# A retention block and a SoLU layer on one core: the state decays once every second chunk, and one written order replaces start, loop and end

## The chip, the core and the metric

The kernel runs on one core of one Trainium2 chip. The core has a matrix engine (PE, whose weight loads are shown apart as PEld), a vector engine (DVE), an activation engine (ACT), a general engine (POOL) and a queue engine (SP), which here issues nearly all DMAs. Each engine works through its own instructions strictly in the order in which they were written; engines wait for one another by semaphores. The metric is the device time of one execution in microseconds (us). The time before is the median of three runs, 217.87 us (217.39 to 219.24).

## What is computed

```python
def _attn_ref(q, k, v):                      # 8 batches, 8 heads, 576 tokens, 64 wide
    scores = scale * np.matmul(q, k.transpose(0, 1, 3, 2))
    gamma = 1.0 - 2.0 ** (-5.0 - np.arange(H, dtype=np.float32))
    Dmat = np.where(rel >= 0, gamma[:, None, None] ** rel[None, :, :], 0.0)
    return np.matmul(scores * Dmat[None, :, :, :], v)
...
def _moe_ref(x, w_in, w_out, g_ln):          # x: 4608 x 512, w_in: 512 x 1024
    h = x @ w_in
    sm = softmax(h)                          # over the 1024
    solu = h * sm
    ln = (solu - mean) / np.sqrt(var + 1e-06) * g_ln
    return ln @ w_out
```

(The softmax is written out in the reference with its maximum, exponential and sum.) All inputs and the output are float32.

## The kernel before

**Tiles.** The 4608 tokens are 36 chunks of 128. A group of nine chunks serves two batches: chunks 0 to 7 of a group are four chunks of each batch, taken in turn, and the ninth holds the last 64 tokens of both. So chunk n has the place c = (n mod 9) // 2 in its batch, and c = 4 for the ninth. The retention is computed chunk by chunk: scores inside the chunk, under a mask, plus the product of the queries with a state that is carried from chunk to chunk of the same batch. The powers of gamma are not put on the scores: q is multiplied by gamma to the position and v by gamma to minus the position (tables in `small`), so that their product has gamma to the distance, and the mask is only a triangle of ones. Positions are counted inside the chunk, so the state has to be multiplied by gamma to the 128 whenever a chunk is passed.

**Steps.** The work on chunk n is cut into named steps. A token `mx:1` in the order calls step `mx` for chunk 1; a letter behind it chooses an engine (`a` ACT, `v` DVE, `g` POOL).

- `ld` three loads q, k, v (L185, L192, on SP). `cq` scales q (L210, or L199 for chunk 34), `cv` scales v (L199), `ck` copies k to 16 bits (L171).
- `tq` eight PE transposes of q and k (L232) and `eq` two copies out of PSUM (L171). From chunk 12 on, for c < 4, `tr` turns q alone (L256), `er` copies it, and `kd` turns k by a DMA transpose (L241).
- `sc` scores (L290), `mk` two masked copies `ret` on DVE (L303), `av` scores times v into `x` (L365).
- `kv` the chunk's k-v product (L314), `ad` adds it to the carried state: `t` (a copy at L327 for c = 0, else the sum at L329, on DVE). `dk` on POOL (L341) makes `s16`, the decayed 16-bit state that the next chunk of the batch multiplies with, `d3` on POOL (L353) the decayed 32-bit state `s32` that the next `ad` adds to. `fs` adds q times `s16` into `x` (L380); for c = 0 there is no state and it issues nothing.
- `ex` copies `x` to `xT` (L171). `m1` (or four quarters `mr` for the first two chunks, L400) is `h = x w_in` (L412), eight matmuls of 512 columns. `mx` the negated row maximum on DVE (L422), `xp` the exponential on ACT (L428), `so` the product on DVE (L437), `ce` a centring for the first five chunks (L448, L453), `sq` the sum of squares on ACT.
- `rt` three tiny POOL instructions (L477, then L481 or L483, then the power at L487) that give 1/sqrt(var). `tu` eight PE transposes (L495) with the copy `eu` (L171), or for seven late chunks `du`, a DMA transpose (L500). `m2` eight matmuls with w_out (L515), `st` the scaled copy on ACT (L523) and the store on SP (L528).
- Set-up steps: `li`, `wi` load and convert w_in, `lo`, `wo` w_out, `mm`, `mc`, `ws` subtract its column mean; `c1` makes constants and loads the tables, `wu` is four matmuls on zeros. The last chunk goes in halves (`hm`, `hx`, `hp`, `ho`, `hc`, `ht`, `he`, `hq`, `h2`, `hw`).

**Order.** Nothing is scheduled by a program at this point: the strings START, LOOP (run for i = 7 to 27, numbers counted from i) and END are the order of every engine's queue. BANKS says which of four PSUM bank slots each PE step takes, in the same order; `h` has two slots of its own. A step that takes a slot waits until its last reader is done. The part of START that the prediction walks through begins with `mx:1`:

```
mr:1:1 mr:0:0 mr:0:2 mk:2 ck:4:g mx:1 xp:1 mr:0:1 mr:0:3 av:2 dk:1 mx:0 tq:4 eq:4:a so:1 cv:4:g
ce:1 wu:0:4 fs:2 lo:1 lo:2 cq:3:v sc:4 ex:2:a ck:3:g cv:3:g tu:1 xp:0 mk:4 m1:2 sq:1 tq:3 eu:1:a
...
wo:0:a sq:0 d3:5 av:6 sq:2 mx:5 fs:6 ck:7:g mm:0 m2:1 cq:7:g ld:9 mx:3 eu:0:a rt:2 mc:0:v m2:0
ce:4 cq:8:v ws:3:v rt:0 xp:3 tu:4 ex:6:a ws:7:v ld:10 ws:4:v ck:8:g dk:5 st:1 xp:5 tq:7 sq:4
so:3 eu:4:v ld:11 eq:7:a m2:2 st:0 so:5 tq:8 ce:3 eq:8:a m1:6 ws:1:v ws:0:v cv:7:g sc:7 ws:2:g
```

and the loop is

```
tr:2 so:-1 tu:-2 ld:6 er:2:v m1:0 dk:0 kv:1 eu:-2:a kd:4 ad:1 cv:3:g av:1 mx:0 sc:2 sq:-2 fs:1
ex:1:a rt:-2 cq:4:g xp:0 m2:-2 d3:0 ck:5:g st:-2 mk:2
```

Of the kernel before, what the change touches and what calls it, by code (L numbers as in the profile page):

```python
# [22 lines left out]
START = """
ld:0 ld:1 c1:0 ck:0:g cq:0:v cv:0:v li:3 gt:0 c2:0 tq:0 cq:1:g cv:1:v ld:2 kv:0 ck:1:v tq:1 ad:0
eq:1:a d3:0 cq:2:v cv:2:g li:2 li:0 eq:0:a kv:1 wi:3:1:a sc:1 li:1 mk:1 dk:0 sc:0 ck:2:a ld:4
av:1 wi:3:0:a wi:2:1:g fs:1 tq:2 ld:3 mk:0 ad:1 av:0 ex:1:a wi:0:0:g eq:2:a fs:0 wi:1:1:a kv:2
mr:1:3 ad:2 d3:1 wi:1:0:g wi:2:0:v cq:4:g wi:0:1:v d3:2 sc:2 mr:1:0 ex:0:v ld:5 mr:1:2 ld:6  # L30
mr:1:1 mr:0:0 mr:0:2 mk:2 ck:4:g mx:1 xp:1 mr:0:1 mr:0:3 av:2 dk:1 mx:0 tq:4 eq:4:a so:1 cv:4:g
ce:1 wu:0:4 fs:2 lo:1 lo:2 cq:3:v sc:4 ex:2:a ck:3:g cv:3:g tu:1 xp:0 mk:4 m1:2 sq:1 tq:3 eu:1:a
dk:2 kv:4 eq:3:a ck:5:a kv:3 av:4 cq:5:g so:0 fs:4 ad:3 d3:3 sc:3 mx:2 dk:3 cq:6:g ex:4:a mk:3
ad:4 tq:5 cv:5:g xp:2 eq:5:a m1:4 lo:0 lo:3 sc:5 d3:4 so:2 cv:6:g mk:5 dk:4 kv:5 av:3 ck:6:a
fs:3 tq:6 d3:6 wo:4:g av:5 ex:3:a ld:7 eq:6:a wo:1:g mx:4 ad:5 wo:7:g kv:6 xp:4 m1:3 fs:5 ce:0
ce:2 wo:2:a ex:5:a tu:0 tu:2 sc:6 wo:5:a m1:5 ld:8 ad:6 so:4 wo:3:a eu:2:v mk:6 rt:1 wo:6:v
wo:0:a sq:0 d3:5 av:6 sq:2 mx:5 fs:6 ck:7:g mm:0 m2:1 cq:7:g ld:9 mx:3 eu:0:a rt:2 mc:0:v m2:0
ce:4 cq:8:v ws:3:v rt:0 xp:3 tu:4 ex:6:a ws:7:v ld:10 ws:4:v ck:8:g dk:5 st:1 xp:5 tq:7 sq:4
so:3 eu:4:v ld:11 eq:7:a m2:2 st:0 so:5 tq:8 ce:3 eq:8:a m1:6 ws:1:v ws:0:v cv:7:g sc:7 ws:2:g
tu:3 st:2 rt:4 ws:5:v ld:12 m2:4 mk:7 sc:8 sq:3 eu:3:a cq:9:g mx:6 mk:8 m2:3 st:4 dk:6 rt:3  # L40
cq:10:g kv:7 ck:9:a ws:6:v xp:6 cv:9:v ad:7 cv:8:v st:3 av:7 fs:7 ex:7:a ck:10:a ck:11:a
"""
# [4 lines left out]
END = """
d3:-7 tr:-5 kd:-3 cq:-3:g kv:-6 av:-6 er:-5:v ld:-1 ad:-6 tr:-4 fs:-6 ex:-6:a dk:-7 sq:-9
so:-8 sc:-5 m1:-7 cv:-4:g er:-4:v mk:-5 tr:-3 kd:0 kv:-5 ck:-2:g av:-5 sq:-8 fs:-5 tu:-8 mx:-7
ad:-5 rt:-9 cv:-3:g dk:-5 er:-3:a tu:-9 kd:-2 m1:-6 xp:-7 sc:-4 kv:-4 cq:-2:v eu:-9:v so:-7  # L50
ex:-5:a m1:-5 sc:-3 mk:-4 rt:-8 du:-7 d3:-6 ld:0 mx:-6 eu:-8:a d3:-5 mk:-3 ad:-4 ck:-1:a dk:-6
m2:-9 av:-4 mx:-5 xp:-6 kv:-3 av:-3 d3:-4 cv:-1:g st:-9 d3:-1 ad:-3 kd:-1 cv:-2:g d3:-2 cq:0:g
fs:-4 fs:-3 so:-6 tr:-2 er:-2:v ex:-4:a xp:-5 m2:-8 sq:-6 dk:-4 sc:-2 mk:-2 ck:0:g m1:-4 so:-5
kv:-2 kv:-1 du:-5 ex:-3:a av:-2 sq:-7 st:-8 mx:-4 sq:-5 xp:-4 fs:-2 m1:-3 cq:-1:v cv:0:g kq:-1
rt:-5 dk:-3 ex:-2:a d3:-3 ad:-2 du:-6 tr:0 so:-4 er:0:a m2:-7 sc:0 m1:-2 ad:-1 mk:0 mx:-3
sc:-1 rt:-6 mk:-1 mx:-2 m2:-5 sq:-4 du:-4 kv:0 rt:-7 rt:-4 av:-1 av:0 fs:-1 dk:-1 m2:-6 st:-7
xp:-3 so:-3 ex:-1:v xp:-2 so:-2 du:-3 du:-2 dk:-2 sq:-3 st:-6 fs:0 m1:-1 rt:-3 ex:0:a st:-5
sq:-2 hm:0:0 hm:0:1 m2:-3 mx:-1 hx:0:0 hx:0:1 xp:-1 hp:0:1 so:-1 m2:-2 hp:0:0 ho:0:1 ho:0:0
du:-1 ht:0:1 hc:0 st:-3 ht:0:0 m2:-4 he:0:1:v sq:-1 hq:0:0:v he:0:0:v rt:-2 rt:-1 ad:0
hq:0:1:a h2:0:0 rt:0 m2:-1 h2:0:1 st:-4 st:-2 hw:0:0:a st:-1 hw:0:1:v  # L60
"""
# [32 lines left out]
def kernel(  # L94
# [61 lines left out]
    gq, gk = small[:, 0:8], small[:, 8:16]  # L156
    gqt, gkt = small[:, 16:24], small[:, 24:32]
    gs = small[:, 32:36]
    gd = small[:, 36:44].rearrange("p (a b) -> p a b", a=4)
    gqm = small[:, 44:52]  # L160
# [43 lines left out]

    def cq(n, e="g"):
        if not quads(n):
            return scaled(n, "qf", "q16", gq, ENG[e])
        table = gqm if chunks[n][1] == 4 else gqt
        dst = half.tile([P, H, D], F16, name="q16", bufs=5)
        ENG[e].tensor_tensor(  # L210
            out=dst.rearrange("p (a h) d -> p h a d", h=2),
            in0=T.pop(("qf", n)).rearrange("p (h a) d -> p h a d", h=2),
            in1=table.rearrange("p (h a) -> p h a", h=2).unsqueeze(3).to_broadcast([P, 2, 4, D]),
            op=ALU.mult,
        )
        T["q16", n] = dst
# [88 lines left out]

    def kv(n):

        k16, v16 = T.pop(("k16", n)), T["v16", n]
        if chunks[n][1] == 4:
            return  # L310
        kp = bank([P, 4, D], FP, "kp")
        for hp in range(4):
# [5 lines left out]
        T["kp", n] = kp

    def ad(n):  # L320
# [1 line left out]
        if chunks[n][1] == 4:  # L322
            return
        (b,), c = chunks[n]
        t = stp.tile([P, 4, D], FP, name="t")
        if c == 0:
            nc.vector.tensor_copy(out=t, in_=T.pop(("kp", n)))  # L327
        else:
            nc.vector.tensor_tensor(  # L329
                out=t, in0=T.pop(("kp", n)), in1=T.pop(("s32", b, c)), op=ALU.add  # L330
            )
        T["t", n] = t

    def dk(n):

# [4 lines left out]
        s16 = stp.tile([P, 4, 2, D], F16, tag=f"s16_{b % 2}", name="s16")  # L340
        nc.gpsimd.tensor_tensor(  # L341
            out=s16, in0=t.unsqueeze(2).to_broadcast([P, 4, 2, D]),
            in1=gd.unsqueeze(3).to_broadcast([P, 4, 2, D]), op=ALU.mult,
        )
        T["s16", b, c + 1] = s16

    def d3(n):

        if chunks[n][1] >= 3:
            return  # L350
        (b,), c = chunks[n]
        s32 = stp.tile([P, 4, D], FP, tag=f"s32_{b % 2}", name="s32")
# [4 lines left out]

    def av(n):

        ret, v16 = T.pop(("ret", n)), T.pop(("v16", n))  # L360
        x = bank([P, 4, P], FP, "x")

        for hp in range(4):
            for e in range(2):
# [5 lines left out]
        T["x", n] = x  # L370

    def fs(n):

        bs, c = chunks[n]
        qkT = T.pop(("qkT", n))
        s16 = [T.pop(("s16", b, c)) for b in bs] if c > 0 else []
        w = P // len(bs)
        for hp in range(4):
            for i, s in enumerate(s16):
# [88 lines left out]
            )  # L468
        T["ss", n] = ss

    def rt(n):

        w1 = tiny.tile([P, 1], FP, name="w1")
        w2 = tiny.tile([P, 1], FP, name="w2")
        rs = tiny.tile([P, 1], FP, name="rs")
        s = T.pop(("s", n))
        nc.gpsimd.tensor_scalar(  # L477
            out=w1, in0=s, scalar1=s, scalar2=1e-6 * DFF, op0=ALU.mult, op1=ALU.mult
        )
        if n < PLAIN:  # L480
            nc.gpsimd.tensor_tensor(out=w2, in0=w1, in1=T.pop(("ss", n)), op=ALU.add)  # L481
        else:
            nc.gpsimd.tensor_scalar(  # L483
                out=w2, in0=T.pop(("ss", n)), scalar1=1.0 / DFF**2, scalar2=w1, op0=ALU.mult,
                op1=ALU.add,
            )
# [248 lines left out]
    def run(order, base):  # L735

        for token in order.split():
            name, n, *more = token.split(":")
            n = base + int(n)
            if 0 <= n < NCH:  # L740
                step[name](n, *more)

    with tc.manual_schedule():
        run(START, 0)
        for i in range(FIRST, STOP - STEP + 1, STEP):
            run(LOOP, i)
        run(END, NCH - 1)


# [28 lines left out]
```

## Time and profile before

| | us |
|---|---|
| three runs: median (lowest to highest) | 217.87 (217.39 to 219.24) |
| the profiled execution: its own time | 218.18 |
| its span in the profile | 216.5 |
| PE busy, share of the span | 197.4, 91% |
| DVE busy | 180.8, 84% |
| POOL busy | 173.6, 80% |
| ACT busy | 167.1, 77% |

The profile is of one execution. Its own time is 1.7 us longer than the span, which runs from the first to the last instruction. Busy time is the union of an engine's instructions; on DVE, ACT and PE an instruction starts a little before the one ahead of it has ended, so the step from one start to the next is shorter than the duration (a DVE maximum lasts 1.22 us and the next instruction starts 1.14 us after it). In a timeline each row has its start, its duration, the engine, the line, the operation and what is written and read.

### The profile page before, as it was taken

The page shows a single profiled execution, that of the slowest core. Times are in us where ns is not written, and L with a number is a line of the kernel's source. Part 1 is how long each engine was busy: PE and PEld are TensorE (multiplying, and loading weights), DVE is VectorE, ACT ScalarE, POOL GpSimd, SP SyncE. Part 2 cuts the span into 40 slices and gives each one's busy share as a digit, 9 for nine tenths or more (in the row PEclk, how much of TensorE's full clock was granted, in tenths as well). Part 3 has the DMA queues.
Part 4 walks back from the last instruction along what each step waited for, and adds up shares of the span by engine and source line. Part 5 has one row for each costly group of instructions (what it writes and reads, how often), then busy time and mean ns, then how long its engine had stood idle before and what let it go on. Part 6 is the DMA issues. An engine that isn't in the chain of part 4 may idle for free.

```text
span 216.5 us, 5376 instructions
## 1 busy us (share of the span) xinstructions
PE 197.4 (91%) x1989; PEld 110.8 (51%) x1989; DVE 180.8 (84%) x289; ACT 167.1 (77%) x279; POOL 173.6 (80%) x275
## 2 busy tenths in 40 slices
PE   0379889896999999999999999999999999999993
PEld 0254456453455555555555555555555565545451
DVE  1378899999997998888888898888888999889840
ACT  2073988966897888888888788888888794986991
POOL 3348889997367899999997899999997899977340
PEclk9999999999999999999999999999999999999999
DMA  5999999998986899799999998899999999674845
GB/s 137 289 317 287 228 280 358 193 245 224 270 228 168 219 183 201 177 225 258 243 223 232 255 208 186 186 247 248 214 227 213 253 181 190 145 172 100 195 109 182
DMA packets 112250, 47.04 MB, mean 217 GB/s; under 512 B 96984, under 2 KB 106208, under 8 KB 112224
## 3 DMA queue, kind: packets, MB, share of 16 engines
q1 hardware_dynamic: 111904, 46.55, 92.7%
q8 instruction: 15, 0.25, 0.5%
q10 hardware_dynamic: 320, 0.16, 0.3%
q14 instruction: 11, 0.09, 0.2%
HBM read 32.54 MB, written 9.44 MB: 194 GB/s over the span
## 4 chain that ended last, share of the span: by engine, by line
PE 78%; DVE 13%; DMA 2%; issue 2%; SPq 2%; ACT 1%; DVEq 0%; ACTq 0%
PE o L515 26%; PE h L412 23%; PE sc L290 5%; PE lp L495 5%; PE x L365 4%; PE x L380 3%; PE kp L314 3%; DVE nm L422 3%; DVE ret L303 2%; DMA vf<-in_v_dram 2%; PE tp L232 2%; PE tr L256 2%; PE h L400 2%; DVE u L437 2%; DVE q L210 1%
## 5 line engine op out<-in xcount | busy, mean ns | idle before, releaser
L412 PE MATMUL h<-w_in,xT 128*128 128x512 f16 x264 | 62.4, 379 | 0.5 <-DVE u L437 0.5
L515 PE MATMUL o<-w_c,uT 128*128 128x512 f16 x240 | 56.5, 379 | 0.6 <-DVE t L327 0.4
L428 ACT ACTIVATE e<-h,nm 128x1024 f32<-128x1024 f32 x35 | 39.0, 1116 | 14.0 <-DVE nm L422 14.0
L303 DVE TENSOR_TENSOR ret<-sc,tris 128x512 f16<-128x512 f32 x72 | 46.1, 682 | 1.3 <-PE sc L290 1.2
L437 DVE SCALAR_TENSOR_TENSOR u<-h,e 128x1024 f16<-128x1024 f32 x35 | 42.7, 1220 | 2.7 <-ACT e L428 1.4
L422 DVE TENSOR_REDUCE nm<-h 128x1 f32<-128x1024 f32 x35 | 42.5, 1216 | 2.0 <-PE h L412 1.5
L515 PEld LDWEIGHTS <-uT 128*128 128x128 f16 x280 | 26.2, 98 | 27.1 <-issue 0.4
L412 PEld LDWEIGHTS <-xT 128*128 128x128 f16 x264 | 24.2, 98 | 24.4 <-issue 0.5
L341 POOL TENSOR_TENSOR s<-t,small 128x512 f16<-128x512 f32 x32 | 34.2, 1070 | 2.6 <-DVE t L329 2.6
L199 POOL TENSOR_TENSOR v<-vf,small 128x512 f16<-128x512 f32 x32 | 33.6, 1051 | 3.0 <-DMA vf<-in_v_dram 3.0
L465 ACT ACTIVATE sq<-u,su 128x1024 bf16<-128x1024 f16 x30 | 34.8, 1159 | 0.1
L210 POOL TENSOR_TENSOR q<-qf,small 128x512 f16<-128x512 f32 x30 | 31.3, 1044 | 1.8 <-DMA qf<-in_q_dram 1.8
L171 ACT CAST xT<-x 128x512 f16<-128x512 f32 x34 | 19.9, 585 | 11.1 <-PE x L380 10.6
L523 ACT ACTIVATE o_sb<-o,rs 128x512 f32<-128x512 f32 x35 | 23.9, 685 | 4.1 <-POOL rs L487 1.6
L171 ACT COPY uT<-lp 128x1024 f16<-128x1024 f16 x25 | 25.3, 1012 | 0.3 <-PE lp L495 0.2
L487 POOL TENSOR_TENSOR rs<-w,mhalf 128x1 f32<-128x1 f32 x36 | 19.8, 551 | 3.0
L483 POOL TENSOR_SCALAR w<-ss,w 128x1 f32<-128x1 f32 x31 | 8.9, 287 | 15.9 <-ACT sq L465 13.9
L171 POOL CAST k<-kf 128x512 f16<-128x512 f32 x28 | 17.1, 611 | 3.0 <-DMA kf<-in_k_dram 3.0
L171 ACT COPY qkT<-tp 128x512 f16<-128x512 f16 x20 | 10.7, 594 | 10.9 <-PE tp L232 10.9
L495 PE MATMUL lp<-ident,u 128*128 128x128 f16 x224 | 17.0, 219 | 1.3 <-DVE u L453 1.3
L353 POOL TENSOR_TENSOR s<-t,small 128x256 f32<-128x256 f32 x24 | 14.9, 622 | 3.4 <-DVE t L327 2.5
L290 PE MATMUL sc<-qkT 64*128 64x128 f16 x288 | 15.2, 225 | 2.0 <-ACT qkT L171 1.2
(89 smaller groups left out, 262.5 us busy)
## 6 DMA issues: line engine op xcount, KB each, us to landing
qf<-in_q_dram SPq DMA_DIRECT2D x32, 256.0 KB, 4.0
kf<-in_k_dram SPq DMA_DIRECT2D x32, 256.0 KB, 4.4
vf<-in_v_dram SPq DMA_DIRECT2D x32, 256.0 KB, 4.7
out_dram<-o_sb SPq DMA_DIRECT2D x32, 256.0 KB, 2.6
w_in<-in_moe_w_in_dram SPq DMA_DIRECT2D x4, 512.0 KB, 6.1
w_out<-in_moe_w_out_dram SPq DMA_DIRECT2D x4, 512.0 KB, 6.7
qf<-in_q_dram SPq DMA_DIRECT2D x8, 128.0 KB, 3.2
kf<-in_k_dram SPq DMA_DIRECT2D x8, 128.0 KB, 3.8
```

The lines of the kernel that those rows point to most:

```text
L171: (engine.copy if engine is nc.scalar else engine.tensor_copy)(out=out, in_=in_)
L199: engine.tensor_tensor(out=dst, in0=T.pop((key, n)), in1=table.unsqueeze(2).to_broadcast([P, H, D]), op=ALU.mult,)
L210: ENG[e].tensor_tensor(out=dst.rearrange("p (a h) d -> p h a d", h=2), in0=T.pop(("qf", n)).rearrange("p (h a) d -> p h a d", h=2), in1=ta ...
L303: nc.vector.tensor_tensor(out=r, in0=s, in1=m, op=ALU.mult)
L341: nc.gpsimd.tensor_tensor(out=s16, in0=t.unsqueeze(2).to_broadcast([P, 4, 2, D]), in1=gd.unsqueeze(3).to_broadcast([P, 4, 2, D]), op=ALU.mult,
L412: nc.tensor.matmul(out=h[:, i * 512 : (i + 1) * 512], lhsT=xT[:, d], rhs=w_in16[:, d, i * 512 : (i + 1) * 512], start=d == 0, stop=d == 3,)
L422: nc.vector.tensor_reduce(out=nm, in_=T["h", n], axis=AX.X, op=ALU.max, negate=True)
L428: nc.scalar.activation(out=e, in_=T["h", n], func=ACT.Exp, bias=T.pop(("nm", n)), accum_out=s)
L437: nc.vector.scalar_tensor_tensor(out=u, in0=T.pop(("h", n)), scalar=-1.0, in1=T.pop(("e", n)), op0=ALU.mult, op1=ALU.mult, accum_out=su,)
L465: nc.scalar.activation(out=s, in_=T.pop(("v", n)), func=ACT.Square, scale=-float(DFF), bias=T.pop(("su", n)), accum_out=ss,)
L495: nc.tensor.transpose(out=lp[:, c], in_=u[:, c * P : (c + 1) * P], identity=ident)
L515: nc.tensor.matmul(out=o, lhsT=uT[:, c], rhs=w[:, c], start=c == 0, stop=c == NF - 1)
```

## The change

- The tables hold three sets of powers (even chunk of a pair, odd chunk, last half chunk): the exponents of two neighbouring chunks are counted from one common origin, from -128 to -1 in the first and from 0 to 127 in the second. `small` grows from 52 to 100 columns.
- So the 32-bit state is decayed only after the second chunk of a pair, by gamma to the 256: `d3` issues an instruction only for c = 1, and after c = 0 and c = 2 the sum `t` itself is the carried state. `dk` stays for every chunk and multiplies with 1, gamma^256, 1 or gamma^128. `t` gets four buffers in place of two.
- `rt` is split: `ra` (its first two tiny instructions, on POOL or, for chunks 0, 3, 6, 7, 12, 22 and 28, on DVE) and `rp` (the power, on POOL).
- `fs` is still empty for c = 0, and `ex` no longer waits for its place in the order there.
- One string ORDER, without loop, takes the place of START, LOOP and END, with its own BANKS. Every PE step stays; copies are dealt out to engines anew.

```diff
-START = """
...
-LOOP = """
...
-END = """
...
+ORDER = """
+ld:0 c1:0 cq:0:v cv:0:g ld:1 cq:1:g ld:2 ck:0:a tq:0 eq:0:a sc:0 cq:2:g ck:1:a tq:1 wu:0:4 eq:1:a
+gt:0 cv:1:v ck:2:g cv:2:g tq:2 mk:0 av:0 ex:0:a eq:2:va li:0 wi:0:0:g kv:1 ad:1 kv:0 ad:0 c2:0
+sc:1 li:2 kv:2 li:3 wi:3:0:g li:1 wi:1:0:g mk:1 ad:2 wi:0:1:a mr:0:0 sc:2 mk:2 ld:4 cq:4:g av:1
+ex:1:a wi:2:0:v wi:2:1:v wi:3:1:a mr:1:3 mr:1:0 mr:1:2 wi:1:1:a mr:1:1 mx:1 mr:0:2 ck:4:a dk:2
+dk:0 mr:0:1 mr:0:3 mx:0 tq:4 av:2 fs:2 ld:3 cv:4:g xp:1 so:1 cq:3:g d3:2 ce:1 eq:4:a sc:4 ex:2:a
+m1:2 xp:0 cv:3:g ck:3:a mk:4 sq:1 so:0 ld:5 tq:3 eq:3:av av:4 cq:5:g kv:3 ad:3 fs:4 ex:4:a tu:1
+ld:6 mx:2 eu:1:a ck:5:g sc:3 mk:3 ce:0 xp:2 so:2 tq:5 dk:3 lo:0 eq:5:a dk:1 m1:4 av:3 fs:3 lo:2
+tu:0 ck:6:a lo:1 cq:6:g ex:3:a tq:6 ra:1:g sc:5 eu:0:a mx:4 d3:3 m1:3 cv:5:g mk:5 cv:6:g av:5 fs:5
+rp:1 kv:4 xp:4 eq:6:a ex:5:a wo:5:a lo:3 ce:2 so:4 ad:4 tu:2 eu:2:a wo:0:a wo:2:a ld:7 wo:1:g sc:6
+ce:4 wo:3:a mk:6 wo:6:v m1:5 ld:8 ld:9 kv:5 sq:2 kv:6 ad:6 wo:4:g dk:4 mx:5 wo:7:g av:6 ad:5 fs:6
+ex:6:a dk:6 xp:5 sq:0 tu:4 mx:3 m2:1 m2:2 cq:7:g ld:12 ra:2:g cq:8:v rp:2 ld:13 mm:0 st:2 so:5
+eu:4:v ck:7:g tq:7 mc:0:v ck:8:g m2:0 ra:0:v st:1 ws:0:v eq:7:v tq:8 xp:3 so:3 dk:5 ce:3 cq:9:g
+sq:5 sc:7 mk:7 ra:5:g rp:0 st:0 m1:6 tu:3 eq:8:a sc:8 ws:2:g ld:10 m2:4 mx:6 rp:5 mk:8 sq:4 ck:9:a
+cv:7:g kv:7 ws:3:v ad:7 eu:3:a sq:3 av:7 fs:7 ld:11 xp:6 ra:3:v ra:4:g rp:4 ex:7:a tu:5 cv:12:g
...
+ck:30:v kd:30 tr:30 eu:25:a er:30:a cq:32:v m1:27 av:28 ex:28:a mx:27 sc:29 xp:27 sq:26 rp:25
+m2:25 st:25 mk:29 cq:31:g so:27 sq:27 ra:27:g sc:30 m1:28 mk:30 kv:30 av:29 ck:34:g rp:27 ad:30
+d3:30 kv:29 av:30 fs:30 ad:29 dk:29 tr:31 ex:30:a fs:29 mx:28 tu:26 ex:29:a tu:27 xp:28 m1:29
+kd:31 er:31:v eu:26:a sc:31 eu:27:v so:28 mk:31 dk:30 kv:32 ra:26:g mx:29 rp:26 ad:32 tr:32
...
+st:30 av:34 fs:34 xp:33 sq:32 ex:34:v ra:32:g du:32 fs:35 ex:35:a m2:29 so:33 du:33 sq:33 ra:29:g
+ra:33:g m1:34 mx:34 xp:34 hm:35:0 hm:35:1 hx:35:0 rp:33 hx:35:1 du:31 so:34 du:34 rp:29 st:29
+hp:35:1 ho:35:1 m2:32 hp:35:0 rp:32 ho:35:0 m2:33 st:32 ra:31:g sq:34 ra:34:g rp:31 ht:35:1
+ht:35:0 rp:34 hc:35 hq:35:0:v hq:35:1:a m2:31 ra:35:g rp:35 st:31 he:35:1:v st:33 he:35:0:v
+h2:35:0 hw:35:0:a m2:34 st:34 h2:35:1 hw:35:1:v
 """
...
-    gq = (g[None, :] ** p[:, None]) / 8.0
-    gk = g[None, :] ** (-p[:, None])
+    by_token = [g[None, :] ** e[:, None] for e in (p - 128, p, p % 64)]
+    by_four = [g[head] ** e for e in (at - 128, at, at % 64)]
+    gq = [x / 8.0 for x in by_four + by_token]
+    gk = [1.0 / x for x in by_token]
...
-    small = const.tile([P, 52], FP, name="small")
+    small = const.tile([P, 100], FP, name="small")
...
+    def frame(n):
+
+        return 2 if chunks[n][1] == 4 else chunks[n][1] % 2
...
-        t = stp.tile([P, 4, D], FP, name="t")
+        t = stp.tile([P, 4, D], FP, name="t", bufs=4)
...
         T["t", n] = t
+        if c % 2 == 0:
+            T["s32", b, c + 1] = t
...
-            in1=gd.unsqueeze(3).to_broadcast([P, 4, 2, D]), op=ALU.mult,
+            in1=gd[(0, 1, 0, 2)[c]].unsqueeze(3).to_broadcast([P, 4, 2, D]), op=ALU.mult,
...
     def d3(n):
 
-        if chunks[n][1] >= 3:
+        if chunks[n][1] != 1:
             return
...
-    def rt(n):
+    def ra(n, e="g"):
...
-        nc.gpsimd.tensor_tensor(out=rs, in0=w2, in1=mhalf, op=ALU.pow)
+        T["w2", n] = w2
+
+    def rp(n):
+
+        rs = tiny.tile([P, 1], FP, name="rs")
+        nc.gpsimd.tensor_tensor(out=rs, in0=T.pop(("w2", n)), in1=mhalf, op=ALU.pow)
         T["rs", n] = rs
```

More of the change, by code (lines that the diff above doesn't have):

```diff
@@ L32 @@
[L32 to L37, printed above, removed]
@@ L54 @@
[L54 to L59, printed above, removed]
@@ L155 @@
     w_out16 = const.tile([P, NF, DM], F16, name="w_out16")
[L156 to L160, printed above, removed]
+    gq4 = [small[:, 8 * i : 8 * i + 8] for i in range(3)]
+    gq = [small[:, 24 + 8 * i : 32 + 8 * i] for i in range(3)]
+    gk = [small[:, 48 + 8 * i : 56 + 8 * i] for i in range(3)]
+    gs = small[:, 72:76]
+    gd = [
+        small[:, 76 + 8 * i : 84 + 8 * i].rearrange("p (a b) -> p a b", a=4) for i in range(3)
+    ]
+    def frame(n):
+        return 2 if chunks[n][1] == 4 else chunks[n][1] % 2
     banks = iter("".join(BANKS.split()))
@@ L206, in cq @@
         if not quads(n):
-            return scaled(n, "qf", "q16", gq, ENG[e])
-        table = gqm if chunks[n][1] == 4 else gqt
+            return scaled(n, "qf", "q16", gq[frame(n)], ENG[e])
+        table = gq4[frame(n)]
         dst = half.tile([P, H, D], F16, name="q16", bufs=5)
@@ L223, in cv @@
     def cv(n, e="g"):
-        scaled(n, "vf", "v16", gkt if chunks[n][1] == 4 else gk, ENG[e])
+        scaled(n, "vf", "v16", gk[frame(n)], ENG[e])
     def tq(n):
@@ L306, in kv @@
     def kv(n):
-        k16, v16 = T.pop(("k16", n)), T["v16", n]
+        k16, v16 = T["k16", n], T["v16", n]
         if chunks[n][1] == 4:
@@ L369, in av @@
                 )
-        T["x", n] = x
+        T["xs" if chunks[n][1] == 0 else "x", n] = x
     def fs(n):
         bs, c = chunks[n]
-        qkT = T.pop(("qkT", n))
-        s16 = [T.pop(("s16", b, c)) for b in bs] if c > 0 else []
+        if c == 0:
+            return
+        qkT = T["qkT", n]
+        s16 = [T.pop(("s16", b, c)) for b in bs]
         w = P // len(bs)
@@ L738, in run @@
             name, n, *more = token.split(":")
-            n = base + int(n)
-            if 0 <= n < NCH:
-                step[name](n, *more)
+            step[name](base + int(n), *more)
     with tc.manual_schedule():
[L744 to L747, printed above, removed]
+        run(ORDER, 0)
 _INS = ['q', 'k', 'v', 'moe_w_in', 'moe_w_out', 'moe_g_ln']
```

94 lines of the change are left out of this document (56 added, 38 removed).

## The prediction

> **What bounds the kernel now.** I read the busy sums first, then the span cut at three times, then the chain of waits around the cuts, then the timelines of DVE, POOL and PE for prices.
>
> ```profile
> PE 197.4 (91%) x1989; PEld 110.8 (51%) x1989; DVE 180.8 (84%) x289; ACT 167.1 (77%) x279; POOL 173.6 (80%) x275
> ```
>
> No engine but PE is near the span, yet these are means. The stages (columns: window, length, then busy time and count of PE, PEld, DVE, ACT, POOL, clock, DMA share, GB/s):
>
> ```profile
> 0.00:20.65 20.65, 10.77 (x98) 6.37 (x99) 10.01 (x20) 7.17 (x12) 9.52 (x22) 1.00 1.01 257
> 20.65:52.05 31.40, 26.68 (x272) 15.34 (x271) 30.70 (x46) 25.49 (x45) 29.33 (x40) 1.00 1.02 254
> 52.05:212.80 160.75, 159.97 (x1620) 89.08 (x1619) 139.65 (x223) 134.49 (x222) 134.70 (x215) 1.00 0.92 207
> 212.80:216.50 3.70, 0.00 (x0) 0.00 (x0) 0.48 (x1) 0.00 (x0) 0.00 (x0) 1.00 0.39 118
> ```
>
> The reader is to see three stages and a tail. Up to 20.65 (start of the first `mx`) all engines wait for loads: DMA share is full. From 20.65 to 52.05 DVE is busy 30.7 of 31.4 us. From 52.05 to 212.8 PE is busy all but 0.8 us. The hand-over is in the chain (start, us, what), and the last wait of any length on PE is the same one (engine, waited for, total, times, longest):
>
> ```profile
> 51.40 0.61 DVE uT L171
> 52.01 0.04 issue
> 52.05 0.61 PE tp L232 x8
> ```
>
> ```profile
> PE tp L232 <- DVE uT L171: 1.9, 1, 1.9
> PE o L515 <- DVE t L327: 0.4, 1, 0.4
> PE tr L256 <- DVE qkT L171: 0.2, 1, 0.2
> ```
>
> So time is won or lost by how much DVE work stands ahead of how much PE work at the start. Inside the long stage other engines have room, POOL least: its `cv` instructions start at 83.31, 88.71, 94.10 and 99.50, every 5.4 us, while PE passes a chunk in 5.25.
>
> **The change part by part.**
>
> *The state decay.* `d3` issues 8 instructions in place of 24:
>
> ```profile
> L353 POOL TENSOR_TENSOR s<-t,small 128x256 f32<-128x256 f32 x24 | 14.9, 622 | 3.4 <-DVE t L327 2.5 <-DVE t L329 0.8
> ```
>
> 16 x 0.62 = 10 us off POOL, and the loop's 5.4 falls to some 4.8 where c = 0 or 2. PE has only one wait there that follows from POOL's lag (0.4 at 121.1, on `t`), so it is worth 0 to 0.4; I take 0.4. DVE's wait for `dk` to free `t` (0.59 per loop turn) goes with four buffers; beside PE, nothing. A `t` that lives on until the next `ad` costs nothing: of four buffers two are carried.
>
> *Tables.* 26 KB landed 1.6 us after an issue at 0.8, and the first reader starts at 4.55 with the load of q. Twice the size lands by 4.0 if all of it scales: 0, at worst 0.5 if it comes behind q.
>
> *`rt` split, copies dealt anew.* By steps from start to start (uT on DVE 0.60, xT 0.60, turned q 0.60 or 0.48 per half, v 0.61, k 0.33, a tiny instruction about 0.15): DVE gains 8 uT, 4 xT, 3 v, 4 k and 7 pairs of tiny instructions, 4.8 + 2.4 + 1.8 + 1.3 + 2.0, and loses 9.9 of turned q: some 2.4 us more. ACT's sum rises by 1.5, POOL's falls by 22 with the 9 k copies that leave it. In the long stage DVE had 139.65 busy of 160.75, so 2.4 are covered; uncovered they are the price. `rp` on POOL can now wait for DVE; behind it in POOL's queue stand the next chunks' `cq` and `cv`, which have the freed 4 to 5% of room.
>
> *PE.* Every PE step and instruction stays (`fs` was empty for c = 0 already): 0.
>
> *The start, first part: when the first `mx` begins.* Both orders put on SP, ahead of all else, loads of chunks 0 to 2 and four pieces of w_in, 4.46 MB, and end with piece 1. Before, ACT and POOL got that piece at 19.0. Then one cast (0.62) and the last two quarter matmuls (0.43 to 0.97): 20.1 to 20.6. I take 20.2, since three other quarters are now ahead of it and no `sc` lies between; a gain of 0.45 (0 to 0.55).
>
> *The start, second part: DVE's work until PE leads.* Counted from the orders, priced start to start: `mx` 1.14, `so` 1.16, `ce` 0.90 (mean of five), `mk` 1.20, `ad` 0.34, uT 0.60, q 0.61, w_out 1.22, warm 0.60, w_c 0.45.
> Before, `mx:1` to `eu:4`: 6 `mx`, 5 `so`, 4 `ce`, 4 `mk`, 4 `ad`, 2 uT, 2 q, 1 w_out, 1 warm, 3 w_c = 28.0. It took 31.4; the other 3.4 are crowded rows (below) and 0.7 idle.
> After, `mx:1` to `mk:8`, for whose PSUM slot `kv:7` waits: 7 `mx`, 6 `so`, 5 `ce`, 6 `mk`, 4 `ad`, 1 uT, 1 q, 1 w_out, 1 warm, 1 w_c, 3 halves of turned q (1.44), 1 tiny pair = 33.2.
> For the excess: a q on DVE beside POOL and one alone:
>
> ```profile
> 25.27 1.08 POOL L199 TENSOR_TENSOR v<-vf,small 128x512 f16<-128x512 f32 x1 [0.31 <-DMA vf<-in_v_dram]
> 25.37 1.53 DVE L210 TENSOR_TENSOR q<-qf,small 128x512 f16<-128x512 f32 x1
> ...
> 176.22 0.68 DVE L210 TENSOR_TENSOR q<-qf,small 128x512 f16<-128x512 f32 x1
> 176.22 0.81 POOL L483 TENSOR_SCALAR w<-ss,w 128x1 f32<-128x1 f32 x1
> ```
>
> The first stepped 1.45, as did the other in this stage; one of the two is now POOL's (`cq:3`), so 3.4 - 0.84 = 2.6 (1.2 if POOL happens not to be in the way, 4.0 if the second `mx` waits as for cold matmuls, below). `mk:8` ends at 20.2 + 33.2 + 2.6 = 56.0.
> What PE has left, at 1.73 per `m1` or `m2`, 0.33 `sc`, 0.34 `av`, 0.45 `tu`, 0.22 `tr` and `fs`, 0.185 `kv`, 0.45 or 0.22 per eight or four transposes: before, from `tq:8`, 156.9, which took 160.75 (3.85 more: 0.09 where a `kv` follows an `m1`, small gaps, and 0.8 idle). After, from `kv:7`, 151.9. End of PE: 56.0 + 151.9 + 3.85 - 0.4 = 211.35, against 212.8: 1.45 earlier. The extra 5.2 of DVE work buys 5.0 of PE work, so nearly all of the gain is the earlier start, one crowded q and the one wait.
>
> *Late steps.* `kd:31` now stands behind `st:25` on SP and just before `sc:31`. From the end of `m2:25` PE has 6.4 us of work until `sc:31`; ACT's 0.69, a store's 0.6 and the transpose's 4.2 to landing make 5.5. Covered by 0.9; if its issue (up to 1.84 seen) comes on top, 0.9 late. `dk:20` (1.07) stands just ahead of `fs:22`; POOL's room hides it. Loads are moved far (`ld:29` ahead of `ld:21`), all at least 4.8 us of PE work ahead of their readers after chunk 6, against 4.7 to landing: 0, up to 1.
>
> *The tail.* The last tokens are the same two half products, store and two half copies: 3.7 again (3.5 to 4.0).
>
> Sum: span 216.5 - 1.45 = 215.05; own time of the profiled execution 218.18 - 1.45 = 216.7. That execution was 0.3 above the median of its runs, so against 217.87 the forecast is 216.4.
>
> Where two instructions crowd, the Trainium skill's page "SBUF — State Buffer" (section "SBUF: two separate sides") says that DVE, with two SBUF inputs or in a two-port mode, and GpSimd hold a shared port pair as an exclusive lock for a whole instruction, and the other blocks. By that rule, against the change, each SBUF-only DVE step could wait for a whole POOL instruction (1.04); the trace agrees that one side blocks, but at 176.22 POOL was the one (0.81 where its like takes 0.27). By the rule alone the 13 steps of the third rival below would cost 13.5 in place of 10.9, and the sum would be 225.2; by the mean of the w_c rows (0.23) they cost 3.0 and the sum stays.
>
> **The rivals.**
>
> *More is won (214.5).* If no DVE step is crowded in the start, the excess is 1.2, not 2.6, and PE's 0.8 idle and 0.15 of tail go as well: 1.45 + 1.4 + 0.55 = 3.4. For it: POOL was busy 29.3 of 31.4 us there and loses four `d3`. Against: it gets `cv:0`, `cq:1`, `cq:3`, and the pricing leaves little idle.
>
> *Nothing is won (217.9).* First `mx` at 20.6, excess 3.4: 0.05 gained, 0.15 lost by the counts. For it: the loads bound the first part in both, and POOL's work was beside PE. The change then does not do what it says for the time.
>
> *Crowding moves into the long stage (222).* Between `mk:8` and `mk:18`, 13 SBUF-only steps stand on DVE (6 w_c, 4 tiny pairs, a k, a q, a v). By `mk:18` DVE's steps sum to 90.8, 12.3 us of idle lie before the first `mx` and 2.6 of excess behind: 105.7, while PE reaches the `m2:14` that waits for its slot at some 110.4. So 4.7 us are to spare. At 0.84 each the 13 cost 10.9, 6.2 over: 216.4 + 6.2 = 222.6. It decides from 0.36 per step; w_c rows lost 0.23 on average (0.41 alone, 0.68 crowded), which speaks against it.
>
> *Cold matmuls (217.8).* At 17.2 two 512-column matmuls took 0.97 (0.485 each), at 18.75 fourteen took 3.61 (0.258), later eight take 1.73 (0.216), though the clock row shows 9 throughout. If the quarters of chunk 0 all go at 0.485, the second `mx` waits 1.4 longer: 216.4 + 1.4. The new order leaves PE more gaps before 19 us, which speaks for it. The Trainium skill, "TensorE: Matmul & The Clock Gate" (section "What's actually happening"), has half rate until about 3.4 us of sustained work; it would make this case likelier, and the two rates of the trace agree with it.
>
> **How the numbers follow.** A measurement of this kernel tells about 1% (2.2 us) from no change: faster means under 215.7, slower above 220.05. Chances: forecast (215.5 to 217.2) 0.36, more won 0.27, nothing won or cold (217.2 to 219.5) 0.22, crowding or late transposes and loads 0.15, nearly all of it above 220. Faster: 0.27 and a twelfth of the forecast's, 0.30. Slower 0.14. Same 0.56. The likeliest alone spans 215.5 to 217.2; eight in ten lie from 213.4 (1.1 below the case in which more is won: DVE's excess gone whole) to 220.
>
> **What would show it.** Right: first `mx` near 20.2; DVE over 95% busy from there to some 56; PE busy all but 1 us from there to some 211; L353 eight times; POOL near 150 busy; a tail of 3.7. Wrong: a PE wait on DVE after 60, a second `mx` more than 1 us behind the first's end, `sc` waiting for a DMA transpose, or DVE idle over 2 us between 21 and 56.

## The result, and the profile after

The changed kernel took 224.53 us (median of four runs, 224.33 to 224.79), the kernel before 218.56 beside it on the same chip: a ratio of 1.030 (95% interval 1.026 to 1.034), slower by 6 us, where 216.4 was forecast and 213.4 to 220.0 given as the range. The profiled execution took 224.33, with a span of 222.3.

The busy sums of the page:

```profile
PE 201.9 (91%) x1989; PEld 111.3 (50%) x1989; DVE 184.4 (83%) x305; ACT 168.3 (76%) x289; POOL 155.3 (70%) x233
```

POOL lost 18 us (22 were forecast), and `d3` issues what it should (columns: group, count, busy, mean ns, idle before):

```profile
L390 POOL TENSOR_TENSOR s<-t,small 128x256 f32<-128x256 f32 x8 | 4.9, 612 | 0.1
```

The cuts of the prediction, laid at the same events in the changed kernel (start of the first `mx`, end of `mk:8`, end of PE; columns as before):

```profile
0.00:21.67 21.67, 13.56 (x104) 6.89 (x105) 8.40 (x17) 8.50 (x14) 11.22 (x23) 1.00 1.03 264
21.67:56.02 34.35, 31.89 (x330) 18.12 (x328) 32.97 (x56) 29.64 (x51) 29.67 (x39) 1.00 0.99 257
56.02:218.60 162.58, 156.50 (x1560) 86.27 (x1556) 142.58 (x232) 129.97 (x225) 114.39 (x173) 1.00 0.87 197
218.60:222.30 3.70, 0.00 (x0) 0.00 (x0) 0.48 (x1) 0.20 (x1) 0.00 (x0) 1.00 0.46 141
```

The reader is to see that the first two stages end at 56.02, where the forecast had 56.0, and that the tail is 3.7. The loss is in the third: 162.58 us where 155.35 (151.9 + 3.85 - 0.4) were forecast, with PE idle for 6.1 of them instead of 0.8. The waits of PE name what it idles for:

```profile
PE sc L325 <- DMA qkT<-k: 2.4, 4, 1.0
PE sc L325 <- ACT qkT L206: 2.3, 2, 1.2
PE x L402 <- DVE ret L338: 0.9, 3, 0.4
PE o L558 <- DVE w_c L773: 0.7, 1, 0.7
```

The first line had no counterpart before: four scores wait for the DMA transpose of k. It accounts for 2.4 us only, so waits alone don't explain the loss. I therefore follow one number through each kernel: PE's *lag*, the start of a PE step less all the PE work that the order puts ahead of it, at the prices of the prediction. Where PE runs without a stop, at its full rate, the lag stands still. By PE work done:

| lag, us, at | 35 us of work | 45 | 75 | 90 | 120 | 150 | end | from 45 to the end |
|---|---|---|---|---|---|---|---|---|
| before | 21.3 | 21.6 | 22.0 | 22.2 | 23.0 | 24.0 | 24.8 | 3.2 |
| after | 19.6 | 21.2 | 22.0 | 24.7 | 26.5 | 29.6 | 30.5 | 9.3 |

So the new start does put PE 1.7 us ahead at 35 us of work, 1.3 of that are gone 10 us of work later, and then the long stage costs 9.3 us in place of 3.2. That is 5.7 in sum (-1.7 + 1.3 + 6.1), against 5.8 between the ends of PE.

One of the late transposes, seen on SyncE's queue. Before (timeline of SP: start, duration, line, operation):

```profile
88.82 1.22 SPq L241 DMA_TRANSPOSE qkT<-k  x1
90.14 0.52 SPq L528 DMA_DIRECT2D out_dram<-o_sb  x1
90.71 0.65 SPq L185 DMA_DIRECT2D qf<-in_q_dram  x1
91.41 0.61 SPq L192 DMA_DIRECT2D kf<-in_k_dram  x1
92.06 0.58 SPq L192 DMA_DIRECT2D vf<-in_v_dram  x1
92.81 1.76 SPq L241 DMA_TRANSPOSE qkT<-k  x1
```

and after, the same two transposes (chunks 15 and 16):

```profile
87.20 2.05 SPq L276 DMA_TRANSPOSE qkT<-k  x1
89.30 1.28 SPq L220 DMA_DIRECT2D qf<-in_q_dram  x2
90.68 1.32 SPq L227 DMA_DIRECT2D kf<-in_k_dram  x2
92.04 1.31 SPq L227 DMA_DIRECT2D vf<-in_v_dram  x2
93.40 0.63 SPq L220 DMA_DIRECT2D qf<-in_q_dram  x1
94.13 0.55 SPq L227 DMA_DIRECT2D kf<-in_k_dram  x1
94.72 0.58 SPq L227 DMA_DIRECT2D vf<-in_v_dram  x1
95.41 2.05 SPq L276 DMA_TRANSPOSE qkT<-k  x1
```

Before, a store and three loads stand between the two transposes; the second is issued at 92.81, has landed at 96.87, and `sc:16` starts at 99.81, 2.9 us later. After, nine loads stand between them (chunk 17's six and chunk 20's three), back to back, with hardly 0.1 us between issues. The chain of waits shows what this does (start, us, what):

```profile
94.52 0.35 DVE nm L461
94.87 0.54 issue
95.41 5.49 DMA qkT<-k
100.90 0.05 issue
100.95 0.40 PE sc L325 x8
```

From issue to landing it took 5.5 us instead of 4.1. Before, in every chunk whose transpose of k has its landing in the trace (19 of 21), it landed 2.6 to 6.1 us ahead of the score. After, it was 0.05 us ahead at chunks 16, 21, 28 and 30, and far ahead at others (13 us at chunk 19): the order has no even lead any more. Counted in PE work from the token `kd` to the end of its `sc`, before has 9 to 12 everywhere, after anything from 0.3 to 21.

### The profile page after: what moved, and what is told of

It is laid out like the page before. It is cut to its first block, busy times and chain, and to the rows that moved or that the text cites. A ratio compares the mean times of both kernels' runs of the same rounds, so it can differ in the third digit from the quotient of the medians.

```text
span 222.3 us, 5338 instructions
## 1 busy us (share of the span) xinstructions
PE 201.9 (91%) x1989; PEld 111.3 (50%) x1989; DVE 184.4 (83%) x305; ACT 168.3 (76%) x289; POOL 155.3 (70%) x233
## 4 chain that ended last, share of the span: by engine, by line
PE 51%; DVE 18%; DMA 12%; SPq 8%; ACT 5%; issue 3%; POOL 1%; DVEq 0%; POOLq 0%
PE o L558 17%; PE h L451 14%; DMA qkT<-k 6%; DVE u L476 4%; DVE ret L338 4%; PE lp L538 3%; PE sc L325 3%; SPq L220 3%; PE x L402 3%; DVE nm L461 3%; SPq L227 3%; PE x L419 2%; DMA qf<-in_q_dram 2%; DMA kf<-in_k_dram 2%; PE h L439 2%
## 5 line engine op out<-in xcount | busy, mean ns | idle before, releaser
L245 POOL TENSOR_TENSOR q<-qf,small 128x512 f16<-128x512 f32 x29 | 32.1, 1111 | 5.6 <-DMA qf<-in_q_dram 5.6
L234 POOL TENSOR_TENSOR v<-vf,small 128x512 f16<-128x512 f32 x29 | 30.3, 1052 | 5.4 <-DMA vf<-in_v_dram 4.5
L206 ACT CAST xT<-x 128x512 f16<-128x512 f32 x30 | 17.4, 588 | 10.6 <-PE x L402 5.5
L521 POOL TENSOR_SCALAR w<-ss,w 128x1 f32<-128x1 f32 x26 | 6.9, 264 | 25.2 <-ACT sq L504 23.7
L530 POOL TENSOR_TENSOR rs<-w,mhalf 128x1 f32<-128x1 f32 x36 | 20.2, 563 | 4.1 <-DVE w L521 2.6
L206 ACT COPY uT<-lp 128x1024 f16<-128x1024 f16 x17 | 17.2, 1014 | 0.8 <-PE lp L538 0.8
L538 PEld LDWEIGHTS <-u 128*128 128x128 f16 x224 | 14.0, 98 | 5.3 <-issue 1.0
L402 PE MATMUL x<-ret,v 128*64 128x128 f16 x288 | 15.6, 227 | 1.1 <-DVE ret L338 0.9
L325 PEld LDWEIGHTS <-qkT 64*128 64x128 f16 x288 | 8.7, 97 | 13.5 <-issue 4.3
```

The lines of the kernel that those rows point to most:

```text
L206: (engine.copy if engine is nc.scalar else engine.tensor_copy)(out=out, in_=in_)
L245: ENG[e].tensor_tensor(out=dst.rearrange("p (a h) d -> p h a d", h=2), in0=T.pop(("qf", n)).rearrange("p (h a) d -> p h a d", h=2), in1=ta ...
L325: nc.tensor.matmul(out=s[e][:, hp], lhsT=qkT[dd, 1, hp], rhs=qkT[dd, 0, hp], start=True, stop=True,)
L538: nc.tensor.transpose(out=lp[:, c], in_=u[:, c * P : (c + 1) * P], identity=ident)
```

## The experiments

All carry the ratio to the kernel before, run beside them, with its 95% interval. Growth is that of the lag from 45 us of work to the end (before 3.2, after 9.3), from the profiled execution.

One thing has to be known to read the growths. In five of the changed orders below, PE's granted clock fell to one half for 3.4 us (once for 6.8) in the long stage, each time 1.6 to 3.3 us after the start of a standstill of PE of 1.8 to 3.0 us. The longest `m1` or `m2` in each took 2.8 to 3.6 us in place of 1.73. So a long wait there costs up to 1.7 us (once 2.7) on top of itself, and the growths contain it. The profiled executions of the kernel before and of the changed kernel have no such stretch in the long stage.

### Which part of the change: arithmetic, start, or long stage

The new arithmetic in the order of before:

```diff
 LOOP (and START, END)
-... ex:1:a rt:-2 cq:4:g ...
+... ex:1:a ra:-2:g rp:-2 cq:4:g ...
```

> The order, the banks and every engine choice of before, with only the new arithmetic: three sets of powers, state decayed once every second chunk, four buffers for t. Theory A (SP's queue: what costs time in the changed kernel is that k's DMA transposes and loads stand too late in SP's order, the arithmetic is harmless): 0 to 1 us below before. Theory B (DVE's steps crowd with POOL's after the new division of copies): the same, 0 to 1 us below before, as the division is the old one. If the arithmetic itself costs time (bigger table, longer-lived t): above before by 1 us or more.

218.88 us, ratio 1.008 (1.003 to 1.013), growth 3.3: no gain and no loss worth the name. The 10 us taken off POOL buy nothing that shows.

Then both joins of the two orders at `kv:9`, with new arithmetic: the new start with before's order behind it, and the reverse.

```diff
 ORDER (after)
 ... sq:6 mk:9 m2:5
-kv:9 ex:8:a xp:7 cq:10:g av:9 ...
+cq:10:g ck:10:a ck:11:a ... (before's order, less what is done)
```

> The steps of the changed kernel up to the key-value product of chunk 9 (about the first 43 us of TensorE's work), then the order of the kernel before; the new arithmetic throughout; the PSUM banks are given out anew. If the loss comes from the order of the long stage (theory D), the lag of TensorE behind its own work stays near 19.5 to 20 us where the two orders join and grows by at most 3.5 us from there, as it does before: 215 to 218.5 us. If the loss comes from the new start or from the new arithmetic's buffers (rival), it is over 221 us.

218.70 us, ratio 1.006 (1.002 to 1.011), growth 3.9. The reverse:

```diff
 ORDER (before's START and LOOP, written out)
 ... up to kv:9, then
+av:9 ra:6:v ex:9:a cq:12:g mx:8 tr:12 ld:15 ... (after's order, less what is done)
```

> The mirror: the start of the kernel before up to the same key-value product, then the order of the changed kernel; the new arithmetic throughout; banks given out anew. Theory D: the 9 us that TensorE loses in the long stage of the changed kernel are lost here as well, 223 to 228 us. The rival (start or buffers): 217 to 220 us.

228.80 us, ratio 1.052 (1.042 to 1.062), growth 11.4, of which some 1.7 belong to a stretch at half the clock (104.9 to 108.3 us). So the long stage's order makes the loss, and it makes it behind either start. In the first the lag was 20.2 at 35 us of work, but 22.2 at 45: the start's lead does not outlive the join.

### SyncE's queue, or crowding on SBUF

Theory A: the loss is SyncE's queue, loads and transposes one behind the other. Theory B: the prediction's rival, SBUF-only steps of DVE crowded by POOL.

Transposes earlier (twelve `kd` to at least 10 us of PE work ahead, two `ck` too, six turned tiles):

```diff
-... sc:14 mk:14 m1:13 tr:16 kd:16 xp:12 ...
+... fs:13 sq:10 tr:14 er:14:v kd:16 mx:12 ...
-        T["qkT", n] = att.tile([P, 2, 4, P], F16, name="qkT", bufs=4)
+        T["qkT", n] = att.tile([P, 2, 4, P], F16, name="qkT", bufs=6)
```

> The changed kernel with k's DMA transposes of chunks 14 to 16, 18, 20, 21, 24, 28, 30, 31, 33 and 34 moved ahead in the order to at least 10 us of PE work before their scores (k copies 28 and 30 moved ahead on POOL too), and six buffers for the turned q and k. Theory A: the four direct waits of PE on a transpose (2.4 us, with what precedes them 3.2) go, and with them about as much of later waits: 3 to 6 us below the changed kernel, so 1.00 to 1.02 of before. Theory B: at most 1 us below the changed kernel.

228.99 us, ratio 1.051 (1.037 to 1.065): not faster. Theory A in the form "put the transposes earlier and all is well" fell. That it is slower lies in good part in the clock: in the profiled execution (231.81 us) three stretches at half the clock take some 6 of a growth of 16.3, which leaves about 10, near the changed kernel's 9.3; the mean clock of its other runs was 0.983 to 0.990. Two scores still wait 3.6 us for a transpose there.

The same with the loads from chunk 14 on in order of need and two more buffers for each load (`e4_sp_order`) has no time: it does not fit on the core, since one tile pool needs 12 KB per partition where 10.3 are left.

DVE's tiny pairs to POOL, and from chunk 9 on its scalings too:

```diff
-... ra:6:v ck:10:v ...
+... ra:6:g ck:10:g ...
```

> The changed kernel with all tiny ra steps on POOL, and from chunk 9 on the k copies and the scalings of q and v that were on DVE put on POOL. Theory A: within 1.5 us of the changed kernel. Theory B (13 and more DVE steps on SBUF crowd with POOL and hold DVE up): 3 to 6 us below the changed kernel.

232.63 us, ratio 1.071 (1.059 to 1.083). Theory B in this form forecast 3 to 6 us less than the changed kernel, and it fell: POOL, though it has room on average, is not where these steps can go. This does not clear DVE's steps of crowding; the fourth kernel of the next part prices them.

k turned by PE, no DMA transposes but one:

```diff
-BY_DMA = 12
+BY_DMA = 34
```

> The changed kernel with the keys of chunks 12 to 33 turned by TensorE instead of by a DMA. TensorE gets about 21 x 0.22 = 4.6 us more, ScalarE or VectorE one eviction of some 0.48 us more a chunk, SyncE loses 21 issues of 1.6 us. Theory A (late transposes behind SyncE's loads): the lag grows by 3 to 4 us in the long stage instead of 9.2, so 222.5 to 224.5 us in spite of the added work. Theory B (the SBUF steps of VectorE and GpSimd crowd): the growth of 9 us stays, 228 to 231 us.

227.76 us, ratio 1.049 (1.038 to 1.061), above what A expected and just under what B did. Counting the added 4.6 us as PE work, the growth is 7.0: lower than 9.3, but the evictions are paid by ACT and DVE.

Stores issued by ACT:

```diff
-            nc.sync.dma_start(out=out[b * S + s0 : b * S + s0 + m, :], in_=o_sb[pp])
+            nc.scalar.dma_start(out=out[b * S + s0 : b * S + s0 + m, :], in_=o_sb[pp])
```

> The changed kernel with the stores of the output issued by ScalarE, right behind the step that makes them, instead of by SyncE, whose queue loses 38 issues and the 18 us that it waits for their data. Theory A: transposes and loads come earlier, the growth of the lag in the long stage falls from 9.2 to 4 to 6 us, 219 to 222 us. Theory B, or if ScalarE pays for the issues on the path: 224 to 228 us.

230.05 us, ratio 1.059 (1.050 to 1.067), growth 13.0. No score waits for a DMA any more; the longest waits of its scores are now for ACT, which issues 38 stores between its own steps (PE's waits of this kernel):

```profile
PE sc L324 <- ACT qkT L205: 3.5, 4, 1.2
```

So a SyncE with fewer issues does bring its transposes in time; ACT could not take the issues over.

### Work left out

To price each suspect by itself, the next four leave work out; their outputs are not the reference's. Theory E: it is the compute engines' own order, not the queue.

No loads from chunk 14 on (those chunks scale chunk 13's tiles):

```diff
         for key, src in (("qf", q), ("kf", k), ("vf", v)):
+            if n > 13:
+                T[key, n] = T["kept", key]
+                continue
```

> The changed kernel without the loads of q, k and v from chunk 14 on: those chunks scale chunk 13's tiles, every other step stays. SyncE's queue is left with transposes and stores. Theory A (loads and transposes late behind SyncE's queue): the growth of the lag after 45 us of work falls from 9.2 to about the 3.5 of the kernel before, 218 to 219.5 us. Theory E (the compute engines' own order, each waiting in order for another): 222 to 225 us.

222.00 us, ratio 1.020 (1.011 to 1.029), growth 5.3. All transposes are still issued, and no score waits for one any more.

No transposes of k but the first (the scores from chunk 12 on use chunk 12's turned k, but for the half chunks):

```diff
-        nc.sync.dma_start_transpose(
-            out=T["qkT", n][:, 1], in_=T["k16", n].rearrange("p h d -> p (h d)")
-        )
+        if "kT" not in T:
+            T["kT"] = const.tile([P, 4, P], F16, name="kT")
+            nc.sync.dma_start_transpose(out=T["kT"], in_=T["k16", n].rearrange("p h d -> p (h d)"))
```

> The changed kernel without the DMA transposes of k but the first: chunks 12 to 33 use chunk 12's turned keys, no other work is added. The waits for the transposes (2.4 us directly) go with what they delay. Theory A: 219 to 221.5 us. Theory E: 222 to 224 us.

220.49 us, ratio 1.012 (1.005 to 1.019), growth 5.5. Leaving out either of the two takes the same 3.8 to 4.0 us off the growth (off the medians 2.5 and 4.0 us). No run leaves out both. But without the loads no score waits for a transpose, and from 45 us of work on the lag takes the same course in both kernels, within 0.2 us: as far as this shows, what costs is that they meet. It is also more than the 2.4 us that PE's waits for DMA show; each late score makes VectorE's mask, and what stands behind it, late as well, which would explain the rest. The longest waits of PE on its scores and on `x` in the kernel without transposes:

```profile
PE sc L327 <- ACT qkT L205: 2.3, 2, 1.2
PE x L404 <- DVE ret L340: 0.9, 3, 0.4
```

They are the same two lines as in the changed kernel: only the DMA line is gone.

The control, before's long stage behind the new start (the first join) with the same loads left out:

> Control: the kernel with the new start and the order of before from the key-value product of chunk 9 on, and without the loads from chunk 14 on, as in the first of this call. Its growth of the lag was 3.9 us with loads; both theories expect 3 to 4 without, 217 to 218.7 us, since before's order is ahead of its loads.

219.38 us, ratio 1.009 (1.004 to 1.014), growth 3.8 against 3.9 with loads: before's order loses nothing to its loads.

And the changed kernel without the loads and without the scalings and copies of chunks 14 to 35:

```diff
+        if n > 13:
+            T[out, n] = T["kept", out]
+            T.pop((key, n))
+            return
         dst = half.tile([P, H, D], F16, name=out, bufs=5)
```

> The changed kernel without the loads and without the scalings and copies of q, k and v from chunk 14 on (all use chunk 13's), so that GpSimd has only the state and the small steps, and VectorE and ScalarE lose their share of it. Theory A: as without the loads, 217 to 219.5 us. Theory B (crowding of the SBUF steps) or E by way of GpSimd: what is left above the first of this call goes here, 215 to 218 us. If the growth of 9 us stays even so, the order of the PSUM steps on VectorE and ScalarE alone is at fault, over 222 us.

220.14 us, ratio 1.012 (1.007 to 1.017), growth 4.2: 1.1 less than without the loads alone. So of the 6.1 us between 9.3 and 3.2, 3.9 are the meeting of loads and transposes, 1.1 the input steps on DVE, ACT and POOL, and about 1.0 is left over, at `tr:18` and `tu:14`, where PE takes two chunks' steps together.

### Which of the two is badly placed, or is the queue full?

Loads at before's lead (9.7 us of PE work ahead of their first reader), nothing else:

```diff
-... m1:10 dk:9 ld:19 kv:11 ad:11 ...
+... rp:9 dk:12 ld:19 ld:20 ex:12:a ...
```

> The changed kernel with the loads from chunk 14 on put where before has them, 9.7 us of TensorE's work ahead of the first step that reads them, in that order (in the changed kernel from 1.7 to 31 us ahead); nothing else moves. If it is the loads issued too early that hold SyncE's queue ahead of the transposes (theory A, load side), most of the 3.9 us that went with the loads come back: 219.5 to 222 us. If the transposes' own places are at fault (5 us ahead of their use at 20, 28 and 30, 0.3 at 31), the time stays within 223.5 to 226 us.

228.53 us, ratio 1.051 (1.044 to 1.057), above both expectations. The growth is 12.1, some 1.7 of it in a stretch at half the clock, and three scores now wait 4.8 us for a transpose: loads in even order do not help while the transposes stay where they are.

The same, and all transposes at least 10 us of work ahead, with six turned tiles:

```diff
-... m1:13 tr:16 kd:16 xp:12 ...
+... tr:14 er:14:v kd:16 mx:12 ...
```

> The one above, and the transposes at least 10 us of TensorE's work ahead of their scores (with the copies of chunks 24, 28 and 30 ahead of them, and six turned tiles instead of four). Theory A in full: both halves of the queue in order, 219 to 221.5 us, the waits of the scores for a DMA gone. If SyncE's queue is short of room rather than badly ordered (theory S), an earlier transpose only delays loads: 224 to 229 us, as with the transposes alone.

228.56 us, ratio 1.053 (1.045 to 1.060). Here no score waits for a DMA, and yet the growth is 13.8 (some 3.2 of it in two stretches at half the clock). PE's waits, and DVE's timeline at the longest:

```profile
PE x L401 <- DVE ret L337: 4.1, 6, 2.5
PE tr L290 <- ACT o_sb L565: 2.2, 1, 2.2
```

```profile
96.08 0.68 DVE L205 CAST xT<-x 128x512 f16<-128x512 f32 x1
101.06 0.69 DVE L233 TENSOR_TENSOR v<-vf,small 128x512 f16<-128x512 f32 x1 [4.30 <-DMA vf<-in_v_dram]
101.67 1.28 DVE L337 TENSOR_TENSOR ret<-sc,tris 128x512 f16<-128x512 f32 x2
```

DVE stands still for 4.3 us for the v of chunk 17, while the mask of chunk 15, which PE needs at once, stands behind it in its queue. The changed kernel has no such wait: in both, DVE's only other wait for v is the 4.7 us for the first one at the start. What a transpose gains in SyncE's queue a load loses.

Late transposes put into the sound order (the first join above, with `kd` moved towards the leads of the changed kernel: chunks 16, 18, 20, 24, 28, 30, 31 and 33 now have 4 to 8 us of PE work to the end of their score instead of 9 to 11):

```diff
-... kv:13 eu:10:a kd:16 ad:13 ...
+... ld:19 er:15:v kd:16 m1:13 ...
```

> The fault put into a sound order: the kernel with the new start and before's order from the key-value product of chunk 9 on, with ten of its transposes put as late ahead of their scores as the changed kernel has them (4 to 8 us of TensorE's work instead of 9 to 11). If late places alone make the loss (theory A, transpose side): 221 to 225 us, with waits of the scores for a DMA. If such a transpose is late only behind loads that run ahead (load side): 218.5 to 220 us.

225.63 us, ratio 1.034 (1.024 to 1.044), growth 7.7 against 3.9, with PE's wait back:

```profile
PE sc L324 <- DMA qkT<-k: 4.4, 4, 1.5
```

That is 3.8 us from late `kd` tokens alone, in an order that has no loads running ahead, and with the full clock through the whole long stage. So late places suffice for a loss of this size. In the changed kernel no run mended them by themselves. Its scalings are ordered far ahead (`cq:18` before `cq:14`, `ck:29` at chunk 18), so that earlier transposes make its loads late, as the v of chunk 17 shows. Two things stay open. SyncE's queue and the 16 DMA engines behind it are both nearly full here (DMA share 0.88 to 1.07 from 60 to 180 us in either kernel), and no run loaded the one without the other; that the stores moved to ACT's queue ended the waits for transposes at the same traffic speaks for the queue. And the last 1.0 us was located, but not tried.

No run here beats the kernel before: even without loads and scalings the changed order grows by 4.2.

## Why the prediction was wrong

- *State decay: right in what it removes, 0.4 too much in what it is worth.* 16 of 24 instructions went; alone they changed nothing (ratio 1.008).
- *Start, first part: wrong by 1.5.* The first `mx` began at 21.67, not 20.2. The four quarter products of chunk 1 began at 18.17 and stepped 0.89, 0.85, 0.86 and 0.70 us; at 0.43, as in the first join, the `mx` would have begun at 20.1. The loads did not hold it: the last piece of w_in was there at 18.1, earlier than the 19.0 that I had taken over. It is the rival of cold matmuls, which I had put at chunk 0 and not at chunk 1.
- *Start, second part: right in the end, 56.02 for 56.0, by two misses that cancel, which is luck.* DVE's counted 33.2 us took 34.35: the excess was 1.15, at the lower end given (1.2), not 2.6.
- *PE from there on: this is the step that failed.* I took before's 3.85 us of losses over to an order in which they were not the same losses. They came out as 10.7 (162.58 - 151.9).
- *Late steps: tested at the wrong place.* `kd:31`, the latest by its token, was covered as forecast (it landed 2.0 ahead of `sc:31`). But the issue of a transpose was read too small there: "up to 1.84 seen" is up to 3.41 in the trace of before (the transpose at 159.01). And the loads' least lead, 4.8, leaves out the last chunk's, 1.7. The ones that hurt, 16, 21, 28 and 30, I had not followed through SyncE's queue: I measured loads against their readers ("0, up to 1"), never against the transposes behind them. That meeting in the queue was worth 3.9. The sign was on the list of what would show the forecast wrong: `sc` waiting for a DMA transpose.
- *Crowding: the rival came true in a small part.* Three w_c steps, beside POOL's `dk` and a scaled q, took 2.96 us where I had priced three at 1.35. `m2:5` waited 0.7 for the last of them, and the maximum and the mask behind them were late as well. This is in the chain, and the lag jumps there, by 1.1 at `kv:9` behind that `m2:5` and by 0.45 at `m1:8`: nearly all of its rise from 19.6 to 21.2 between 35 and 45 us of work. It was not tried alone:

```profile
59.71 2.96 DVE w_c L773 x3
62.67 1.14 DVE nm L461
63.81 1.21 DVE ret L338 x2
```

- DVE's 2.4 us more came out as 3.6 (184.4 for 180.8). I called them covered. They were not tried by themselves; all scalings and copies of q, k and v from chunk 14 on, moved or not, cost 1.1. The tail was 3.7, as forecast.
- The rival "crowding or late transposes and loads" had the right sign and a chance of 0.15. Its time, 222.6, was worked out for crowding alone; the mechanism that decided had no price of its own.

## What to carry to other kernels

When an order by hand is rewritten, follow every queue as a queue, SyncE's too: for each DMA that a bounding engine waits for, add up the issues that now stand ahead of it, whatever they are for. Ask for the lead of each in the bound engine's work, and be wary when a narrow band (9 to 12) becomes a wide one (0.3 to 21), even if the mean is the same. The idle time that a page books to a wait can be less than what the wait costs (2.4 and 3.9 us here): leave the work out once to learn its price. And look at the clock in short windows before two orders are compared: a standstill of 2 us can cost 1.7 us on top of itself.

## What the runs showed of the hardware

- In the rows above an issue holds SyncE for 0.52 to 0.66 us a load or store, and for 1.2 to 2.05 us a transpose; between 87.2 and 97.4 us of the changed kernel it issued without a gap over 0.11 us.
- TensorE's rate in the first 25 us differs between kernels with the same order up to there. In the changed kernel, and without loads or without transposes, quarter products stepped some 0.85; in the first join, its control and the kernel without input steps 0.43. The clock records of the traces go with the rates: half the clock from 18.7 to 22.1 us without loads and from 15.6 to 22.5 without transposes, the full clock from 12.3 on in the first join. In the changed kernel the first record begins only at 21.3, where its products go over to 0.43, and in the kernel before at 19.7, where they do the same. Ahead of the first record the profile prints 1.00 all the same, so the 1.00 of the first stage, in the cut above and in the prediction's, says nothing of the rate there. The Trainium skill's page "TensorE: Matmul & The Clock Gate" (section "What's actually happening") has half rate until about 3.4 us of sustained work; the two rates agree, and what gives two kernels of the same order different rates here is not shown. It decides little: at 45 us of work the lag was 21.2, 22.3 and 22.3 with the slow rate, and 22.2, 21.7 and 20.2 without.
- In all traces together PE stood still eleven times for 1.7 us or more after the first 25 us. Nine of these standstills were followed, 1.6 to 3.3 us after they began, by half the granted clock for 3.4 us (in one case 6.8); two were not (1.86 us at 50.2 in the kernel before, 2.42 at 171.6 with loads at before's lead). No standstill under 1.6 us was followed by one, and no such stretch came without a standstill before it. For example, with loads and transposes both early PE stood still for 2.51 us from 99.9, and the clock was at half from 103.2 to 106.6. Which standstill brings it is not shown.
- Of the three w_c steps beside POOL, two took 1.26 us, 0.85 over one that ran alone (0.41). The Trainium skill, "SBUF — State Buffer" (section "SBUF: two separate sides"), would have such a step wait for up to a whole POOL instruction (1.09 for `dk`, 1.11 for a scaled q, the means of this kernel); the trace stays under that and comes near.
